# Experts 1 to 7 of a routed layer behind one branch: two arms with different place widths, and tiles with fixed homes

## The chip, the cores and the metric

The kernel runs on one core of one Trainium2 chip. The metric is the device time of one execution in microseconds (us). Three runs of the kernel before gave 397.07, 397.32 and 399.1 us; the median is 397.32 us.

## The reference, cut to what matters

A recurrent attention layer (4 batches, 8 heads, 768 steps, 48 values per head) makes 3072 rows of 384 values. Each row then goes to one of 8 experts, the one with the largest logit:

```python
logits = x @ w_gate                                   # 3072 x 8
expert_idx = np.argmax(logits, axis=1)
gate_w = probs[np.arange(N), expert_idx]              # softmax of the logits
for e in range(8):
    mask = expert_idx == e
    h = np.maximum(x[mask] @ w1[e], 0.0)              # 384 -> 1024
    out[mask] = gate_w[mask, None] * (h @ w2[e])      # 1024 -> 384
```

How many rows an expert gets depends on the data. With the drawn inputs expert 0 gets 394 rows, and the others, sorted, 432, 411, 407, 380, 358, 355 and 335.

## The kernel before, in words

**Attention and routing** (until about 165 us) work through 24 blocks of 128 steps. Each block's rows are ranked within their expert and scattered by POOL into a buffer `xs` in HBM that has a region per expert.

**Expert 0** has 428 places. It is computed in two parts (`Part`, L725), `pa` with 192 places and `pb` with 236. **Experts 1 to 7** are taken in the order of their sorted counts (`sort_experts`, L658), so that the n-th place width in `CAPS` (L32: 428, 464, 432, 416, 408, 392, 384, 384) has to hold the n-th largest count. The program is the same whatever the counts are: it always multiplies all places, and the unused ones hold rows of zeros whose output goes nowhere. `check` (L684) compares the sorted counts with `CAPS` and sets `flag`; where it is set, a slow `general` kernel (L1096) runs behind everything else in an `If` (L1091).

For one expert `load_x` (L916) fetches its rows, `trans_x` (L921) transposes them on PE and splits each value into a high part (ACT) and a low part (DVE), and `mm1` (L943) computes the hidden layer: 8 slices of 128, each 9 matmuls (3 blocks of 384 times high-high, high-low, low-high) whose moving operand is as wide as the expert's places, so 72 matmuls. ACT and DVE then take each slice out of its PSUM bank as a high and a low part (L316, L317); five banks go round. `mm2` (L956) is the second layer, in one of two forms by `shape` (L912):

- **column-wise** (over 384 places): 72 matmuls as wide as the places (L989), the result is output by places, so 12 transposes on PE turn it round (L978), DVE weighs it (L979) and POOL scatters it (L276);
- **row-wise** (384 places, three groups of 128): 24 matmuls for each group (L326), each 384 wide whatever the number of rows, and no transposes behind them.

Before, experts 1 to 5 are column-wise, experts 6 and 7 row-wise. `feed` (L933) splits a piece of weights (`split_piece`, ACT L250, DVE L252) and has SP issue the load of the next piece into one of four staging buffers `wst`.

**Order of the work.** On SP the order is as written, everywhere. On PE, DVE, ACT and POOL it is as written up to L1077, the end of expert 0. From L1078 on a planner orders the instructions of experts 1 to 7 by its own model of time, and may set one of them ahead of what is written before it where its engine would otherwise wait. An engine takes its queue in order. `values_load` (L909, L1085) reads a number from SBUF into a register of an engine: `order` for SP, and `flag` on all five engines, written between `mm1` and `mm2` of expert 7.

The end of expert 0 and the start of expert 1 are, as written:

```python
        for f in range(8):
            pb.mm1(f)
            if f in (1, 4):
                feed(1, f // 3)
        pb.mm2(0)
        trans_x(1)
        feed(1, 2)
        pb.mm2(1)
        feed(1, 3)
    fin = None
    for e in range(1, E):
        expert(e + 2)
```

Of the kernel before, what the change touches and what calls it, by code (L numbers as in the profile page):

```python
# [19 lines left out]
P = 128  # L20
# [9 lines left out]
CAPS = (428, 464, 432, 416, 408, 392, 384, 384)  # L30
NST = 1
# [21 lines left out]
def rwkv_moe_kernel(ctx, tc, rkw, vv, ub, wgp, wg, w1, w2, out):  # L53
# [34 lines left out]
    nth = {"b": 0, "h": 0, "x": 0, "e": 0}  # L88

    def xtile(shape, name):  # L90
        pool, tag = xbanks[nth["x"] % len(xbanks)]
        nth["x"] += 1
        return pool.tile(shape, F32, name=name, tag=tag)
# [96 lines left out]
    flag = const.tile([1, 1], I32, name="flag")  # L190
# [96 lines left out]
    def bank(n, p=P):  # L287
        pool, tag = banks[nth["b"] % len(banks)]
        nth["b"] += 1
        return pool.tile([p, n], F32, name="bank", tag=tag)  # L290

    def h_tiles(n):
        tags = htags[nth["h"] % len(htags)]
        nth["h"] += 1
        if len(tags) == 1:
            t = wk.tile([P, 2, n], F32R, name="hhl", tag=tags[0])
            return t[:, 0, :], t[:, 1, :]
        return [wk.tile([P, n], F32R, name="h" + "hl"[i], tag=g, bufs=wkb.get(g, 2)) for i, g in enumerate(tags)]
# [374 lines left out]
    def check_w():  # L673

        g = sm.tile([RP, NB, NP_ + 1], F32, name="g", tag="g", bufs=1)
        nc.vector.tensor_single_scalar(out=g[:, :, 0:NP_], in_=wtot, scalar=1e3, op=ALU.is_lt)
        nc.vector.tensor_single_scalar(out=g[:, :, NP_:NP_ + 1], in_=chk.unsqueeze(2), scalar=0.0, op=ALU.is_le)
        gm = sm.tile([RP, 1], F32, name="gm", tag="gm", bufs=1)
        nc.vector.tensor_reduce(out=gm, in_=g.rearrange("p n q -> p (n q)"), axis=AX.X, op=ALU.min)
        gb = sm.tile([RP, 1], BF16, name="gb", tag="gb", bufs=1)  # L680
        nc.vector.tensor_copy(gb, gm)
        ch["gb"] = gb

    def check():  # L684
# [12 lines left out]
        any_ = sm.tile([1, 1], F32, name="any", tag="any", bufs=1)  # L697
        nc.vector.tensor_reduce(out=any_, in_=bad, axis=AX.X, op=ALU.max)
# [17 lines left out]
    class Part:  # L716
        def __init__(self, row, rows):
            self.rows = rows
            self.t = ld.tile([rows, 2, XC], F32, name="xg0", tag="rkwt")
            load_rows(self.t, one, row, 2 * rows, rows)  # L720
            x = ld.tile([P, 2, 3, 2 * rows], F32R, name="x0", tag="rkwt")
            self.x = [x[:, i] for i in range(2)]
            self.hs = []
# [187 lines left out]

    def shape(e):  # L912
        n = CAPS[e]
        return (n // P, P) if n <= 3 * P else (4, n // 4)

    def load_x(e):  # L916
        nq, rows = shape(e)
        xg[e] = ld.tile([rows, nq, XC], F32, name="xg", tag="rkwt")
        load_rows(xg[e], eid[e], 0, CAPS[e], rows)

    def trans_x(e):  # L921
        nq, rows = shape(e)
        xh = ld.tile([P, 3, CAPS[e]], F32R, name="xh", tag="rkwt")
        xl = ld.tile([P, 3, CAPS[e]], F32R, name="xl", tag="rkwt")
# [18 lines left out]
    def mm1(e, fin):  # L943
        xh, xl = xhl[e]
        hs = []
        for f in range(8):
            hh, hl = h_tiles(CAPS[e])
            expand(wts[e % 2], f, xh, xl, bank(CAPS[e]), hh, hl)
            hs.append((hh, hl))
            if f == 1 and fin is not None:  # L950
                fin()
            if f in (2, 4, 6):
                feed(e + 1, f // 2 - 1)
        return hs

    def mm2(e, hs):  # L956
        t = xg[e]
        nq, rows = shape(e)
        wt = wts[e % 2]
# [7 lines left out]
        ot = ld.tile([rows, nq, DM], F32, name="ot", tag="rkwt")  # L967
# [14 lines left out]
        for j in range(3):  # L982
            pp = bank(CAPS[e])
# [9 lines left out]
            oT[j] = wk.tile([P, CAPS[e]], F32, name="oT", tag="tmp")  # L993
# [11 lines left out]
    with tc.manual_schedule(engines={ET.PE, ET.DVE, ET.Activation, ET.Pool}):  # L1005
# [11 lines left out]
        psZ = mctx.enter_context(tc.tile_pool(name="psZ", bufs=2, space=PSUM))  # L1017
        banks = [(psZ, "z"), (psZ, "z"), (psW, "w"), (psA, "ap"), (psD, "dp")]
        xbanks[:] = [(psV, "v"), (psX, "tp"), (psX, "tp")]
        nth["x"] = 0  # L1020
        pa.mm1(1)
# [56 lines left out]
    fin = None  # L1078
    for e in range(1, E):
        expert(e + 2)  # L1080
        if e + 1 < E:
            load_x(e + 1)
        hs = mm1(e, fin)
        if e == E - 1:
            bad = nc.values_load(flag[0:1, 0:1], min_val=0, max_val=1)  # L1085
            tc.mark_branch_hint_location("general", "LikelyTaken", [ET.PE, ET.DVE])
        fin = mm2(e, hs)
# [199 lines left out]
```

## Time and profile before

| | us |
|---|---|
| median of 3 runs | 397.32 |
| the profiled execution, its own time | 397.03 |
| span of that execution, first to last instruction | 395.2 |
| PE busy in the span | 376.6 |
| DVE, ACT, POOL busy | 265.9, 233.8, 120.7 |

The span is what the trace shows, and the execution's own time is 1.8 us more. Up to about 165 us no engine alone sets the pace; from there on PE is the engine to look at.

### The profile page before, as it was taken

The page shows a single profiled execution, that of the slowest core. Times are in us where ns is not written, and L with a number is a line of the kernel's source. Part 1 is how long each engine was busy: PE and PEld are TensorE (multiplying, and loading weights), DVE is VectorE, ACT ScalarE, POOL GpSimd, SP SyncE. Part 2 cuts the span into 40 slices and gives each one's busy share as a digit, 9 for nine tenths or more (in the row PEclk, how much of TensorE's full clock was granted, in tenths as well). Part 3 has the DMA queues.
Part 4 walks back from the last instruction along what each step waited for, and adds up shares of the span by engine and source line. Part 5 has one row for each costly group of instructions (what it writes and reads, how often), then busy time and mean ns, then how long its engine had stood idle before and what let it go on. Part 6 is the DMA issues. An engine that isn't in the chain of part 4 may idle for free.

```text
span 395.2 us, 9409 instructions
## 1 busy us (share of the span) xinstructions
PE 376.6 (95%) x3542; PEld 337.3 (85%) x3542; DVE 265.9 (67%) x480; ACT 233.8 (59%) x651; POOL 120.7 (31%) x173
## 2 busy tenths in 40 slices
PE   8798999999998899999999999999999999999994
PEld 6576877777776679898988999999999999999994
DVE  8999899999999986678952661671771762623311
ACT  8899999999999865158543452462452553420200
POOL 5653224775548834001200140030130230312002
PEclk9999999999999999999999999999999999999999
DMA  8999999999921222798937238229228232011001
GB/s 204 205 219 219 283 246 251 230 283 245 245 64 69 96 86 88 194 357 251 294 111 238 80 84 290 81 71 295 80 70 293 80 104 100 18 39 39 18 2 55
DMA packets 30158, 62.04 MB, mean 157 GB/s; under 512 B 4879, under 2 KB 17978, under 8 KB 30108
## 3 DMA queue, kind: packets, MB, share of 16 engines
q1 hardware_dynamic: 25500, 51.92, 48.0%
q0 software_dynamic: 4608, 9.48, 7.5%
q8 instruction: 29, 0.48, 0.6%
q14 instruction: 21, 0.17, 0.1%
HBM read 49.53 MB, written 12.20 MB: 156 GB/s over the span
## 4 chain that ended last, share of the span: by engine, by line
PE 66%; DMA 14%; DVE 11%; ACT 4%; issue 2%; SPq 1%; POOL 0%; POOLq 0%; DVEq 0%; ACTq 0%
PE bank L314 27%; PE bank L989 18%; DMA rkwt<-in_rkw_dram 13%; PE opt L326 10%; DVE at L405 3%; DVE pre L398 2%; DVE suf L382 2%; PE pt L304 2%; PE ap L503 2%; PE op L978 2%; PE yp L539 2%; DVE kh L392 1%; PE lp L553 1%; DMA wst<-in_w_dram 1%; PE yp L516 1%
## 5 line engine op out<-in xcount | busy, mean ns | idle before, releaser
L276 POOL DMA_INDIRECT out_dram<-ot,xg x26 | 30.1, 1156 | 168.9 <-DVE ot L979 126.3
L252 DVE TENSOR_TENSOR w2l<-wst,w2h 128x512 fp32r<-128x512 f32 x48 | 31.0, 683 | 43.6 <-ACT w2h L250 43.6
L314 PE MATMUL bank<-xl,w1h 128*128 128x384 f32 (+5 forms) x168 | 58.7, 352 | 0.0
L314 PE MATMUL bank<-xh,w1l 128*128 128x384 f32 (+5 forms) x168 | 58.4, 350 | 0.0
L314 PE MATMUL bank<-xh,w1h 128*128 128x384 f32 (+5 forms) x168 | 54.1, 354 | 0.0
L316 ACT ACTIVATE hh<-bank 128x384 fp32r<-128x384 f32 (+7 forms) x58 | 26.1, 471 | 37.0 <-PE bank L314 36.5
L376 ACT ACTIVATE at<-ident,ct 128x128 f32<-128x128 f32 x144 | 47.0, 395 | 0.1
L317 DVE SCALAR_TENSOR_TENSOR hl<-bank,hh 128x384 fp32r<-128x384 f32 (+7 forms) x58 | 29.9, 532 | 24.7 <-ACT hh L316 24.4
L349 POOL TENSOR_TENSOR rk<-rkwt 112x512 f32<-112x512 f32 x24 | 31.9, 1330 | 34.9 <-DVE pre L386 28.6
L994 ACT ACTIVATE oT<-bank 128x464 f32<-128x464 f32 (+4 forms) x15 | 7.9, 523 | 48.9 <-PE bank L989 48.9
L503 PE MATMUL ap<-rh,kh 64*128 64x128 f32 (+1 forms) x384 | 27.9, 284 | 7.3 <-DVE rh L359 6.3
L252 DVE TENSOR_TENSOR w1l<-wst,w1h 128x512 fp32r<-128x512 f32 x48 | 31.3, 687 | 4.7 <-ACT w1h L250 4.5
L503 PEld LDWEIGHTS ap<-rh,kh 64*128 64x128 f32 (+1 forms) x384 | 23.3, 187 | 12.6 <-DVE rh L359 9.1
L250 ACT ACTIVATE w1h<-wst 128x512 fp32r<-128x512 f32 x48 | 28.6, 627 | 9.2 <-PE bank L314 4.8
L989 PE MATMUL bank<-hh,w2l 128*128 128x408 f32 (+4 forms) x96 | 34.0, 355 | 0.0
L989 PE MATMUL bank<-hl,w2h 128*128 128x408 f32 (+4 forms) x96 | 33.8, 354 | 0.0
L989 PE MATMUL bank<-hh,w2h 128*128 128x408 f32 (+4 forms) x96 | 33.7, 356 | 0.0
L405 DVE COPY_PREDICATED at<-cmask,ap 128x1024 f32<-128x1024 int32 x24 | 31.6, 1318 | 2.0 <-PE ap L503 1.4
L704 POOL DMA_INDIRECT xs<-xr,pi x24 | 28.4, 1183 | 14.5 <-DVE mx L572 5.5
L382 DVE TENSOR_TENSOR_SCAN suf<-rkwt,sufone 112x520 f32<-112x520 f32 x24 | 31.4, 1307 | 1.4 <-POOL at L364 0.8
L314 PEld LDWEIGHTS bank<-xh,w1l 128*128 128x128 f32 x168 | 31.5, 188 | 0.8
L314 PEld LDWEIGHTS bank<-xl,w1h 128*128 128x128 f32 x168 | 31.4, 188 | 0.7
(173 smaller groups left out, 852.6 us busy)
## 6 DMA issues: line engine op xcount, KB each, us to landing
rkwt<-in_rkw_dram SPq DMA_DIRECT2D x44, 289.5 KB, 9.1
wst<-in_w_dram SPq DMA_DIRECT2D x48, 256.0 KB, 6.6
wst<-in_w_dram SPq DMA_DIRECT2D x16, 768.0 KB, 7.2
vt<-in_vv_dram SPq DMA_DIRECT2D x24, 192.0 KB, 9.1
xg<-xs SPq DMA_DIRECT2D x6, 579.0 KB, 4.7
xs<-zrow SPq DMA_DIRECT2D x8, 289.5 KB, 9.0
rkwt<-in_rkw_dram SPq DMA_DIRECT2D x4, 224.0 KB
xg<-xs SPq DMA_DIRECT2D x1, 675.5 KB
```

The costliest lines, as they stand in the source:

```text
L250: nc.scalar.activation(hi, st[:, cs], AF.Copy)
L252: nc.vector.tensor_tensor(out=lo, in0=st[:, cs], in1=hi.bitcast(F32), op=ALU.subtract)
L276: i = nc.gpsimd.indirect_dma_start(out=out[:, :], out_offset=bass.IndirectOffsetOnAxis(ap=t.bitcast(I32)[:, q, DM + 1:DM + 2], axis=0), in ...
L314: nc.tensor.matmul(hp, a, x[:, j, :], start=(i == 0), stop=(i == 8))
L317: nc.vector.scalar_tensor_tensor(out=hl, in0=hp, scalar=0.0, in1=hh.bitcast(F32), op0=ALU.max, op1=ALU.subtract)
L326: nc.tensor.matmul(op, hs[f][x == "l"][:, cs], w2v(wt, "h" if part == "hl" else "l", f), start=(i == 0), stop=(i == 23))
L349: i = nc.gpsimd.tensor_tensor(out=d["rk"], in0=d["r"], in1=d["k"], op=ALU.mult)
L376: nc.scalar.activation(blk[n]["at"][:, j, q], ident, AF.Copy, scale=blk[n]["ct"][:, head(q, j):head(q, j) + 1])
L382: nc.vector.tensor_tensor_scan(out=suf[:, ::-1], data0=d["w"][:, ::-1], data1=sufone.rearrange("p q c -> p (q c)")[:, ::-1], initial=0.0, ...
L405: nc.vector.copy_predicated(out=d["at"].rearrange("p j q c -> p (j q) c"), mask=cmask.unsqueeze(1).broadcast_to([P, 2 * NP_, C]), data=d[" ...
L503: nc.tensor.matmul(d["ap"][:, j, q, :], d["kh"][rs, q, :], d["rh"][rs, q, :], start=True, stop=True)
L989: nc.tensor.matmul(pp, w, a, start=(i == 0), stop=(i == 23))
```

## The change

`NEAR` is a second list of place widths, smaller than `CAPS`. `check` also compares the sorted counts with `NEAR` and writes a second flag, `far`. Behind expert 0 there is now an `If` with two arms: where some count does not fit, experts 1 to 7 run with `CAPS`, as before; where all fit, they run with `NEAR`. In the second arm experts 5, 6 and 7 (384, 378, 360 places) are row-wise, and row-wise groups have a third of the places. Expert 1's rows are loaded and transposed before the branch, so with 464 places; its `mm1` reads 4 groups of 112 out of 116. Both flags are loaded into registers of all engines before the branch: `far` behind slice 6 of `pb.mm1`, `bad` behind `pb.mm2(0)`. A prefetch hint for PE, DVE and ACT, so far given for the `general` branch, is now given for this branch, directly ahead of it; the `general` branch has none. Since both arms have to find the tiles in the same places, tiles that came from rotating pools (staging, banks, hidden layer, rows, output) now come from `fixed`, which makes each of a ring's tiles once.

The arm that is skipped stands first; with the drawn inputs every count fits `NEAR`, the third one (407) with one place to spare.

```diff
 CAPS = (428, 464, 432, 416, 408, 392, 384, 384)
+NEAR = (428, 448, 424, 408, 396, 384, 378, 360)
...
     def load_piece(e, i):
-        st = wst.tile([P, 1536], F32, name="wst", tag="wst")
+        st = fixed("st", 4, lambda i: wst.tile([P, 1536], F32, name="wst", tag="wst"))
...
+    def fixed(ring, size, make):
+        k = ring, nth[ring] % size
+        nth[ring] += 1
+        if k not in home:
+            home[k] = make(k[1])
+        return home[k]
...
+    def row_tile(rows, *shape, dt=F32, kind=None):
+        n = shape[0] * shape[1]
+        kind = kind or ("rows" if dt == F32 else "cols")
+        t = fixed(kind, {"rows": 3, "cols": 2, "out": 1}[kind], lambda i: ld.tile([P, NW + 2 * NR], dt, name=kind, tag="rkwt"))
+        return t[0:rows, 0:n].rearrange("p (a b) -> p a b", a=shape[0])
...
     def check_w():
 
+        nc.gpsimd.memset(capn, float(1 << 20))
+        for e in range(NST, E):
+            nc.gpsimd.memset(capn[:, e - NST:e - NST + 1], float((NEAR[e] + 1) * E))
...
+        over = sm.tile([1, E], F32, name="over", tag="over", bufs=1)
+        nc.vector.tensor_tensor(out=over, in0=ch["ks"], in1=capn, op=ALU.is_ge)
+        any_ = sm.tile([1, 2], F32, name="any", tag="any", bufs=1)
+        nc.vector.tensor_reduce(out=any_[:, 0:1], in_=bad, axis=AX.X, op=ALU.max)
+        nc.vector.tensor_reduce(out=any_[:, 1:2], in_=over, axis=AX.X, op=ALU.max)
         nc.vector.tensor_copy(flag, any_)
...
     def shape(e):
-        n = CAPS[e]
-        return (n // P, P) if n <= 3 * P else (4, n // 4)
+        n = caps[e]
+        return (3, n // 3) if n <= 3 * P else (4, n // 4)
...
     def mm1(e, fin):
         xh, xl = xhl[e]
+        if caps[e] < CAPS[e] and e == NST:
+            nq, rows = shape(e)
+            xh, xl = (x.rearrange("p j (q r) -> p j q r", q=nq)[:, :, :, 0:rows] for x in (xh, xl))
...
             pb.mm1(f)
             if f in (1, 4):
                 feed(1, f // 3)
+            if f == 6:
+                far = nc.values_load(flag[0:1, 1:2], min_val=0, max_val=1)
         pb.mm2(0)
+        bad = nc.values_load(flag[0:1, 0:1], min_val=0, max_val=1)
         trans_x(1)
         feed(1, 2)
         pb.mm2(1)
         feed(1, 3)
...
+        tc.mark_branch_hint_location("far", "LikelyTaken", [ET.PE, ET.DVE, ET.Activation])
+
+    def experts():
+        fin = None
+        for e in range(1, E):
+            expert(e + 2)
+            if e + 1 < E:
+                load_x(e + 1)
+            hs = mm1(e, fin)
+            fin = mm2(e, hs)
...
+    with tc.If(far > 0, label="far", preferred_fallthrough_block=True) as cmp:
+        experts()
...
+    with cmp.Else():
+        caps[:] = NEAR
+        experts()
     mctx.close()
```

## Rows read from the trace of the kernel before

**Rows 1.** The page: the span, and the chain that ended last, by engine.

```profile
span 395.2 us, 9409 instructions
...
PE 66%; DMA 14%; DVE 11%; ACT 4%; issue 2%; SPq 1%; POOL 0%; POOLq 0%; DVEq 0%; ACTq 0%
```

**Rows 2.** Windows: stretch, length, busy PE, PEld, DVE, ACT, POOL, clock, DMA.

```profile
177.00:189.00 12.00, 11.21 (x68) 10.50 (x68) 9.91 (x20) 9.95 (x19) 1.65 (x1) 1.00 0.89 260
189.00:203.50 14.50, 14.50 (x73) 12.91 (x72) 11.60 (x20) 8.10 (x17) 2.08 (x1) 1.00 0.62 206
```

**Rows 3.** The chain in order of time, experts 1 to 7: start, us, what.

```profile
189.12 8.44 PE bank L314 x40
197.56 0.37 PE pt L304 x4
...
230.04 5.32 PE bank L314 x27
...
260.42 5.12 PE bank L314 x27
...
289.97 5.04 PE bank L314 x27
...
305.39 0.44 PE op L978 x4
...
318.74 4.84 PE bank L314 x27
...
346.89 4.68 PE bank L314 x27
...
377.61 12.14 PE opt L326 x69
```

**Rows 4.** The chain in order of time, end of expert 0.

```profile
182.56 0.62 DVE ort L330
...
183.23 0.62 PE pt L304 x4
183.84 1.10 PE bank L314 x5
184.95 4.17 PE opt L326 x24
```

**Rows 5.** Timeline at the end of expert 0: idle before, releaser in brackets.

```profile
177.60 1.36 ACT L250 ACTIVATE w1h<-wst 128x512 fp32r<-128x512 f32 x2 [0.95 <-DMA wst<-in_w_dram]
...
180.06 0.43 PE L326 MATMUL opt<-w2h,hl 128*118 128x384 f32 x1 [0.25 <-DVE hl L317]
```

**Rows 6.** Line 1091, the branch: ns min/median/max, first and last start (us).

```profile
L1091 SPq EVENT_SEMAPHORE  x9: 17/17/17, 330.1 to 330.7; - x9
...
L1091 SPq COMPARE_BRANCH  x1: 53/53/53, 325.3 to 325.3; - x1
...
L1091 PEldq COMPARE_BRANCH  x1: 482/482/482, 387.1 to 387.1; - x1
L1091 PEldq EVENT_SEMAPHORE  x1: 51/51/51, 389.8 to 389.8; - x1
```

**Rows 7.** DMA queues between 387 and 389.7 us: packets, MB, share.

```profile
q8 instruction: 1, 0.02, 2.7%
```

**Rows 8.** Line 304, window 179 to 184 us, and line 1085: PE's queue.

```profile
L304 PE MATMUL pt<-ident,xg x12: 260/262/319, 181.7 to 183.6; 116*128 116x116 f32 x12
L304 PEldq EVENT_SEMAPHORE  x1: 51/51/51, 180.1 to 180.1; - x1
...
L1085 PEldq TENSOR_LOAD <-flag x1: 539/539/539, 386.4 to 386.4; - x1
```

**Rows 9.** Timeline of SP: the rows of expert 2, and line 270's landing.

```profile
181.94 0.87 SPq L270 DMA_DIRECT2D xg<-xs  x2
...
DMA to landing us min/median/max: 4.7/4.7/4.7
```

**Rows 10.** Timeline of DVE: the low parts of two pieces of weights.

```profile
185.55 1.88 DVE L252 TENSOR_TENSOR w2l<-wst,w2h 128x512 fp32r<-128x512 f32 x3
```

More of the change, by code (lines that the diff above doesn't have):

```diff
@@ L87, in small @@
         return few["t"]
-    nth = {"b": 0, "h": 0, "x": 0, "e": 0}
+    nth = {"b": 0, "h": 0, "x": 0, "e": 0, "rows": 0, "out": 0, "cols": 0, "st": 0, "o": 0}
+    held = []
     def xtile(shape, name):
-        pool, tag = xbanks[nth["x"] % len(xbanks)]
+        i = nth["x"] % len(xbanks)
         nth["x"] += 1
-        return pool.tile(shape, F32, name=name, tag=tag)
+        if not held:
+            return xbanks[i][0].tile(shape, F32, name=name, tag=xbanks[i][1])
+        if len(held) == i + 1:
+            held.append(xbanks[i][0].tile([P, BANK], F32, name="held", tag=xbanks[i][1]))
+        n = shape[1] if len(shape) == 2 else shape[1] * shape[2]
+        t = held[i + 1][0:shape[0], 0:n]
+        return t if len(shape) == 2 else t.rearrange("p (a b) -> p a b", a=shape[1])
     def load(n, part=None):
@@ L189, in rwkv_moe_kernel @@
     early = const.tile([1, 1], F32, name="early")
-    flag = const.tile([1, 1], I32, name="flag")
+    flag = const.tile([1, 2], I32, name="flag")
+    capn = const.tile([1, E], F32, name="capn")
     ebrow = const.tile([1, GB, E], BF16, name="ebrow")
@@ L285, in rwkv_moe_kernel, with bank, make @@
              ("kt", "kt"), ("at",), ("at",)]
[L287 to L290, printed above, removed]
-    def h_tiles(n):
[L293 to L298, printed above, removed]
+    home = {}
+    def fixed(ring, size, make):
[4 more added lines that the diff above has]
+        return home[k]
+    def bank(n):
+        if not held:
+            return banks[0][0].tile([P, n], F32, name="bank", tag=banks[0][1])
+        return fixed("b", len(banks), lambda i: banks[i][0].tile([P, BANK], F32, name="bank", tag=banks[i][1]))[:, 0:n]
+    def h_tiles(n):
+        def make(i):
+            tags = htags[i]
+            if len(tags) == 1:
+                t = wk.tile([P, 2, CMAX], F32R, name="hhl", tag=tags[0])
+                return t[:, 0, :], t[:, 1, :]
+            return [wk.tile([P, CMAX], F32R, name="h" + "hl"[j], tag=g, bufs=wkb.get(g, 2)) for j, g in enumerate(tags)]
+        hh, hl = fixed("h", len(htags), make)
+        return hh[:, 0:n], hl[:, 0:n]
+    def row_tile(rows, *shape, dt=F32, kind=None):
[3 more added lines that the diff above has]
+        return t[0:rows, 0:n].rearrange("p (a b) -> p a b", a=shape[0])
     def transpose_rows(t, nq, rows, xh, xl):
@@ L718, in __init__ @@
             self.rows = rows
-            self.t = ld.tile([rows, 2, XC], F32, name="xg0", tag="rkwt")
+            self.t = row_tile(rows, 2, XC)
             load_rows(self.t, one, row, 2 * rows, rows)
-            x = ld.tile([P, 2, 3, 2 * rows], F32R, name="x0", tag="rkwt")
-            self.x = [x[:, i] for i in range(2)]
+            x = row_tile(P, 6, 2 * rows, dt=F32R)
+            self.x = [x[:, 3 * i:3 * i + 3] for i in range(2)]
             self.hs = []
@@ L965, in ahead @@
                 trans_x(e + 1)
-        ot = ld.tile([rows, nq, DM], F32, name="ot", tag="rkwt")
+        ot = row_tile(rows, nq, DM, kind="out")
         if nq == 3:
@@ L992, in mm2 @@
                     out_tr(j - 1)
-            oT[j] = wk.tile([P, CAPS[e]], F32, name="oT", tag="tmp")
+            oT[j] = fixed("o", 2, out_t)[:, 0:caps[e]]
             nc.scalar.activation(oT[j], pp, AF.Copy)
@@ L1077, in rwkv_moe_kernel, with out_t @@
         feed(1, 3)
[L1078 to L1087, printed above, removed]
+        tc.mark_branch_hint_location("far", "LikelyTaken", [ET.PE, ET.DVE, ET.Activation])
[7 more added lines that the diff above has]
+            fin = mm2(e, hs)
+    def out_t(i):
+        return wk.tile([P, CMAX], F32, name="oT", tag="tmp")
+    for i in range(2):
+        fixed("o", 2, out_t)
+    row_tile(P, 1, 1, kind="out")
+    kept = [(x, x.copy()) for x in (nth, eid, xg, xhl, stg, todo, outs)]
+    with tc.If(far > 0, label="far", preferred_fallthrough_block=True) as cmp:
+        experts()
+    for x, old in kept:
+        if isinstance(x, list):
+            x[:] = old
+        else:
+            x.clear()
+            x.update(old)
+    with cmp.Else():
+        caps[:] = NEAR
+        experts()
     mctx.close()
```

20 lines of the change are left out of this document (10 added, 10 removed).

## The prediction

> **What bounds the kernel now.** I read the page first, for the span and for what the chain that ended last consists of: PE has 66% of it [rows 1]. Then windows over the part that the change touches: in expert 1's first layer PE is busy for all of the 14.50 us at a granted clock of 1.00 (the 2.4 GHz level), while DVE, ACT and the DMA engines have room [rows 2]. Then the chain in order of time: from 189.12 us to the last row-wise matmul, which begins in the stretch at 377.61, it is matmuls and transposes on PE end to end [rows 3]. So experts 1 to 7 are bound by PE, and what they cost is counted in matmuls. The 12 us ahead of them are not: PE idles there in the 177 to 189 us stretch for 12.00 - 11.21 = 0.8 us [rows 2]. Last I read the rows of the only branch that the kernel has today, since the change puts another one in the middle.
>
> **Part 1, narrower places.** The pitch of a matmul is a row's time over its count [rows 3]: 464 columns 8.44 / 40 = 0.211 us, 432: 5.32 / 27 = 0.197, 416: 0.190, 408: 0.187, 392: 0.179, 384: 0.173. Over the columns that is 0.451 to 0.457 ns each, so time goes with the columns, and I take 0.455. Row-wise matmuls are always 384 wide, at 12.14 / 69 = 0.176 us. A column-wise expert has 144 matmuls as wide as its places, a row-wise one 72 such and 72 of 384. Columns saved: expert 1, 144 x 16 = 2304; experts 2 and 3, 144 x 8 = 1152 each; expert 4, 144 x 12 = 1728; expert 5, 1152 (its second layer goes from 392 to 384); expert 6, only its first layer, 72 x 6 = 432; expert 7, 72 x 24 = 1728. Together 9648 columns, at 0.455 ns **4.4 us** less. All of it lies on the path, since PE waits for nothing there. The bounds are 4.3 and 4.5, by the ends of the pitches.
>
> **Part 2, expert 5 row-wise.** Its 12 output transposes go, 0.44 us for four [rows 3]: **1.3 us** less. Its row transposes on the way in fall from 12 to 9 but get wider; four of 108 take 0.37 us [rows 3], so the gain is between nothing and three of them, 0.3 us, and I take nothing, as fewer and wider cancel. The output then leaves by group as for expert 6, beside PE.
>
> **Part 3, what the branch closes off.** Today the planner sets instructions of experts 1 and 2 ahead of the end of expert 0. Five of expert 1's matmuls (1.10 us) run before `pb.mm2(1)` [rows 4]. They now run behind it: moved, not added, as long as PE has no hole in their place. The hole would be the wait for the first transposed block's bank, and I give it 0.2 us (bounds 0 and 0.6, the length of one DVE operation on such a bank, like `ort` [rows 4]). In return two delays go that the planner's early work makes today. ACT waits 0.95 us for a piece of expert 2's weights, so the last slice's low part is late and PE stands 0.25 us [rows 5]. And `ort` starts at 182.56 on DVE although the transposes behind its matmuls run from 181.7 [rows 4, 8]; that is 0.8 us in which DVE works on early weights, and PE's last four transposes wait for it. Together 0.25 + 0.8 - 0.2 = **0.9 us** less (bounds 0 and 1.1).
>
> **Part 4, the branch itself.** Of the branch of today PE's own instruction takes 0.48 us, but from its start at 387.1 to PE's next entry at 389.8 is 2.7 us [rows 6], and one block of instructions is fetched in that time [rows 7]. What covers it is how far PE's queue is ahead of its array. At the end of `pb.mm2(0)`, also 24 matmuls long, the queue stood at the transposes' wait at 180.1 and the first of them ran at 181.7 [rows 8]: 1.6 us ahead. So PE stands for 2.7 - 1.6 = **1.1 us** more. The bounds: nothing, where the queue is further ahead or the hint helps; and 4.8 - 1.6 = 3.2 us if PE's jump costs what SP's does, whose branch at 325.3 is followed by its next entry at 330.1 [rows 6]. I take PE's own row, as the nearest. A gain is excluded, since the branch only adds.
>
> SP, which gets no hint, I charge 4.8 us. It reaches the branch behind the load of expert 2's third piece, whose staging buffer is free when DVE has split expert 1's third piece (1.88 us [rows 10], behind `trans_x`), near 186 us. Behind the branch wait the load of expert 2's rows and then its last piece. The rows are issued near 192 instead of 181.94 and land 4.7 us later [rows 9], near 197. PE wants them, in today's order, behind expert 1's 45th matmul, at 197.56 [rows 3]. So it costs nothing by a hair, and one for one if SP is later.
>
> ACT and DVE, with 4.8 us each at worst, are covered by five PSUM banks: PE first needs one back after 45 matmuls of 448 columns, 45 x 0.204 = 9.2 us. DVE has `ort` (0.62 us) and a piece of weights (1.88) left when PE ends `pb.mm2(1)` [rows 4, 10], and with 4.8 that is 7.3 us. Without that cover PE would stand for the rest. POOL has nothing in expert 1 that anyone waits for.
>
> **Part 5, small things.** Two loads of a flag on each engine: PE's takes 0.54 us [rows 8] and the queue's 1.6 us cover it; on ACT and DVE it runs beside the operation before. Two more operations on DVE in `check` and eight memsets on POOL stand ahead of slices whose banks have the same five-deep cover: nothing. The fixed homes repeat the rings' old sizes (four staging buffers, five banks, ten hidden pairs, three row tiles, two pairs of places), so I see no wait that they add; the single output tile is rewritten half an expert after its scatter. The tail behind the last matmul stays.
>
> **Sum.** Against the profiled execution's own 397.03 us (span 395.2 [rows 1], and 1.8 around it): 397.03 - 4.4 - 1.3 - 0.9 + 1.1 = 391.5. The median of the runs is 0.3 above that execution, so I predict **391.8 us**.
>
> The Trainium skill, "Advanced Engine Details and Errata", section "Control Flow Timing", gives a compare-and-branch about 108 ns. SP's 53 ns and PE's 482 ns for the instruction alone lie on both sides of it, and neither holds the time until the next entry. By that figure alone PE would stand for nothing, and the sum would be 390.7.
>
> **The rivals.**
> - **The branch is free** on PE, because its queue is further ahead or the hint has the block there in time: 391.8 - 1.1 = 390.7, down to 390.0 with the other lower bounds. For it: 24 matmuls of cover; against: the queue was only 1.6 us ahead at the same place [rows 8]. Chance 0.15. By the figure of the Trainium skill ("Advanced Engine Details and Errata", "Control Flow Timing") it would be this case.
> - **The arm starts late on more than one engine.** PE's jump costs as much as SP's (2.1 more), and PE meets the rows or weights of expert 2 late by 1 to 3 us, because the planner's model put them where they would be without the branch's cost: 393.5 to 397. For it: the hair's breadth above. Chance 0.22.
> - **Slower: SP's branch holds the chain.** If SP gets to the branch only when DVE has also split expert 1's fourth piece (behind `ort`, so near 192 us), or its jump waits behind weights in flight, the rows of expert 2 land late and every piece of weights behind them too. What the change saves is 5.5 us net; it turns when they land over 5.5 us behind the place where PE wants them, near 203, and at 207 the time is 401. Against it: that wait needs a buffer order other than the written one. Chance 0.05.
> - **The other arm runs.** Then the widths are as before and only parts 3 and 4 remain: 397.3 + 0.2, no change. The counts of the drawn inputs fit `NEAR`, one of them by a single place. Chance 0.03.
>
> **How the numbers follow.** The forecast's own band, 390.7 to 393.5, has the remaining 0.55. For 8 in 10 the range takes in the free branch down to 390.0 and the late arm up to 395.0. A measurement of this kernel can tell about 0.5%, 2 us, from no change: faster is below 395.3. That holds for the forecast, the free branch and about two thirds of the late arms, 0.85; same gets the rest of these and the other arm, 0.10; slower 0.05.
>
> **What would show it.** Right: first-layer matmuls of 448, 424, 408, 396, 384, 378 and 360 columns at 0.455 ns a column (expert 7's near 0.164 us); L978 with 48 transposes instead of 60; PE without a hole behind the branch but for one of about 1.1 us ahead of expert 1's first matmul; SP silent for several us behind its branch, and no wait of PE for transposed rows of expert 2. Wrong: widths as before; a hole of over 3 us at the branch; PE waiting on banks, rows or weights within expert 1 or 2; or holes later on that fixed homes make.

## The result and the profile after

| | before | after |
|---|---|---|
| median, range (7 runs each) | 397.15 us (396.34 to 399.1) | 401.66 us (399.92 to 403.85) |
| ratio to before, 95% interval | | 1.0105 (1.0071 to 1.014) |
| the profiled execution | 397.03 us, span 395.2 [rows 1] | 400.59 us, span 398.9 |
| end of PE's last matmul | 389.74 us | 393.12 us |

The change made the kernel slower by about 1%, where 391.8 us was predicted. The kernel before took 397.6 us beside the first four experiments and 401.8 to 403.5 us beside the later ones, so kernels are compared by their ratio to the kernel before that was measured beside them, and by stretches of their traces. The attention part varies by some us from one execution to the next; what the change touches is better read from three marks in each trace: the start of the first matmul of `pb.mm1(0)` (expert 0's second part, 236 columns), the start of the last matmul of expert 1's first layer, and PE's end.

| stretch, us | before | after | change | predicted |
|---|---|---|---|---|
| `pb.mm1(0)` to the end of expert 1's first layer | 168.90 to 203.25: 34.35 | 169.98 to 211.31: 41.33 | +6.98 | -0.3 |
| from there to PE's end | to 389.74: 186.49 | to 393.12: 181.81 | -4.68 | -5.2 |
| PE's end to the end of the span | 5.46 | 5.78 | +0.3 | 0 |

The predicted column splits the terms of the prediction: expert 1's first layer loses 72 matmuls x 16 columns x 0.455 ns = 0.5 us, part 3 takes 0.9 and part 4 adds 1.1; the rest of the 5.7 us of parts 1 and 2 lies behind. So the saving behind expert 1 came, and the loss is all in expert 1's first layer. The page says so too. It shows the row of TensorE over 40 slices, and the clock's row below it:

```profile
PE   8798999999998899999939999999999999999994
...
PEclk9999999999999999999969999999999999999999
```

One slice, at 20 x 10 us, has PE at 3 tenths and the clock at 6 tenths. The windows over the same place (columns as in [rows 2]: stretch, length, busy time of PE, PEld, DVE, ACT and POOL, granted clock, DMA share, GB/s) show the hole:

```profile
189.00:203.50 14.50, 10.61 (x53) 9.42 (x51) 8.03 (x14) 4.01 (x9) 2.09 (x1) 0.97 0.69 208
203.50:220.00 16.50, 13.63 (x60) 12.50 (x61) 9.36 (x16) 8.41 (x17) 0.00 (x0) 0.82 0.90 289
...
200.00:203.00 3.00, 0.00 (x0) 0.00 (x0) 0.00 (x0) 0.00 (x0) 0.00 (x0) 0.93 1.03 344
203.00:206.00 3.00, 0.00 (x0) 0.00 (x0) 2.11 (x4) 2.77 (x6) 0.00 (x0) 0.50 1.05 389
206.00:209.00 3.00, 2.63 (x7) 2.37 (x8) 3.00 (x6) 2.64 (x6) 0.00 (x0) 0.50 1.11 357
209.00:210.00 1.00, 1.00 (x5) 0.91 (x5) 1.00 (x3) 0.12 (x1) 0.00 (x0) 0.80 0.94 227
```

Where [rows 2] had PE busy for all of 14.50 us at a clock of 1.00, PE now has 10.61. From 200 to 203 us none of the five compute rows is busy while the DMA engines are full (1.03). And when PE starts again it runs at half clock (0.50, the 1.2 GHz level) until past 209 us. What PE, DVE and ACT waited for stands in their timelines (start, us, engine, line, operation, in brackets the idle time and what ended it), of PE, of DVE and of ACT in turn:

```profile
199.25 0.36 PE L341 MATMUL bank<-cols,w1l 128*128 128x448 f32 x1
206.37 1.11 PE L341 MATMUL bank<-cols,w1h 128*128 128x448 f32 x2 [6.76 <-DVE hl L344]
...
203.89 1.90 DVE L261 TENSOR_TENSOR w2l<-wst,w2h 128x512 fp32r<-128x512 f32 x3 [6.86 <-ACT w2h L259]
205.70 0.62 DVE L344 SCALAR_TENSOR_TENSOR hl<-bank,hh 128x448 fp32r<-128x448 f32 x1
...
194.86 0.52 ACT L343 ACTIVATE hh<-bank 128x448 fp32r<-128x448 f32 x1
203.22 1.67 ACT L259 ACTIVATE w2h<-wst 128x512 fp32r<-128x512 f32 x3 [7.84 <-DMA wst<-in_w_dram]
204.80 0.52 ACT L343 ACTIVATE hh<-bank 128x448 fp32r<-128x448 f32 x1
```

Read from the end: PE has filled the five banks and waits 6.76 us for one. DVE could free it with `hl`, but has ahead of it the low part of a piece of weights, which waits for ACT's high part (6.86 us). ACT stands at that high part, `w2h`, for 7.84 us, because the piece hasn't landed. Slices of expert 1 that PE finished long ago lie behind it in ACT's queue, and `hh` of one of them runs at 204.80, right behind the split. So a piece of **expert 2's** weights, of the second layer, which begins for expert 2 only at 242.87 us, holds **expert 1's** first layer.

Why the piece is late is seen at the branch (L1138), at the order's load behind it (L942) and in SP's timeline; first the rows of line 1138 and of line 942, from 186 to 200 us (ns min/median/max, first and last start):

```profile
L1138 ACTq COMPARE_BRANCH  x1: 68/68/68, 183.9 to 183.9; - x1
L1138 PEldq COMPARE_BRANCH  x1: 393/393/393, 185.4 to 185.4; - x1
L1138 SPq COMPARE_BRANCH  x1: 53/53/53, 187.7 to 187.7; - x1
L1138 DVEq COMPARE_BRANCH  x1: 84/84/84, 188.8 to 188.8; - x1
...
L942 SPq TENSOR_LOAD <-order x1: 1542/1542/1542, 193.2 to 193.2; - x1
```

and SP's timeline:

```profile
187.26 0.38 SPq L248 DMA_DIRECT2D wst<-in_w_dram  x1
195.37 0.89 SPq L279 DMA_DIRECT2D rows<-xs  x2
196.55 0.41 SPq L248 DMA_DIRECT2D wst<-in_w_dram  x1
```

SP's branch begins at 187.7 and its next entry comes at 193.2, 5.5 us later (4.8 in [rows 6]). Expert 2's last piece is issued at 196.55 us and split from 203.22, 6.7 us later. In the kernel before it was the second of these rows, 12.75 us earlier, 1.9 us behind the rows of [rows 9], and ACT split it from 191.38, 7.6 us later. So the load itself is no slower than before; it is issued late. The first row, DVE's, is the last split of expert 2's second piece; it ends at 183.77, and the load goes out right behind it:

```profile
183.09 0.68 DVE L252 TENSOR_TENSOR w1l<-wst,w1h 128x512 fp32r<-128x512 f32 x1
...
183.80 0.40 SPq L239 DMA_DIRECT2D wst<-in_w_dram  x1
```

On PE the branch, which carries a hint, cost nothing. Line 341's row of PE's queue shows the entries behind the branch from 185.8 us, some 0.45 us behind the start of the branch at 185.4, and PE's first matmul of expert 1 runs at 188.46 us right behind the last one of expert 0. So the queue was 3.1 us ahead of the array:

```profile
L341 PEldq EVENT_SEMAPHORE  x5: 51/51/51, 185.8 to 186.2; - x5
```

### The profile page after: what moved, and what is told of

Its sections match the earlier page's. It is cut to its first block, busy times and chain, and to the rows that moved or that the text cites. A ratio compares the mean times of both kernels' runs of the same rounds, so it can differ in the third digit from the quotient of the medians.

```text
span 398.9 us, 9418 instructions
## 1 busy us (share of the span) xinstructions
PE 372.4 (93%) x3527; PEld 334.8 (84%) x3527; DVE 264.9 (66%) x482; ACT 231.7 (58%) x648; POOL 119.6 (30%) x180
## 4 chain that ended last, share of the span: by engine, by line
issue 47%; PE 19%; DVE 16%; POOL 7%; ACT 7%; DMA 2%; POOLq 0%; SPq 0%; DVEq 0%; ACTq 0%; another core or an unknown queue 0%
POOL out_dram L285 6%; PE held L353 4%; PE bank L341 4%; DVE at L432 4%; DVE pre L425 4%; DVE suf L409 3%; PE ap L530 2%; DMA rkwt<-in_rkw_dram 2%; DVE kh L419 2%; ACT at L403 2%; PE lp L580 2%; PE yp L566 1%; PE yq L573 1%; DVE rh L386 1%; PE yp L543 1%
## 5 line engine op out<-in xcount | busy, mean ns | idle before, releaser
L341 PE MATMUL bank<-cols,w1h 128*128 128x192 f32 (+8 forms) x432 | 108.8, 336 | 6.8 <-DVE hl L344 6.8
L341 PEld LDWEIGHTS bank<-cols,w1h 128*128 128x128 f32 x432 | 76.6, 191 | 8.7 <-DVE hl L344 7.1
L285 POOL DMA_INDIRECT out_dram<-out,rows x25 | 29.5, 1178 | 173.6 <-DVE out L1016 62.3
L341 PE MATMUL bank<-cols,w1l 128*128 128x192 f32 (+8 forms) x216 | 71.3, 331 | 0.0
L344 DVE SCALAR_TENSOR_TENSOR hl<-bank,hh 128x192 fp32r<-128x192 f32 (+8 forms) x58 | 29.2, 522 | 25.0 <-ACT hh L343 23.8
L259 ACT ACTIVATE w2h<-wst 128x512 fp32r<-128x512 f32 x48 | 27.9, 626 | 26.3 <-DMA wst<-in_w_dram 15.0
L341 PEld LDWEIGHTS bank<-cols,w1l 128*128 128x128 f32 x216 | 41.2, 191 | 0.6
L425 DVE TENSOR_TENSOR_SCAN pre<-rkwt,pre 112x520 f32<-112x520 f32 x24 | 30.1, 1252 | 0.0
L1026 PE MATMUL bank<-hl,w2h 128*128 128x396 f32 (+3 forms) x78 | 27.4, 354 | 0.0
L1026 PE MATMUL bank<-hh,w2l 128*128 128x396 f32 (+3 forms) x78 | 27.3, 352 | 0.0
```

The lines of the kernel that those rows point to most:

```text
L259: nc.scalar.activation(hi, st[:, cs], AF.Copy)
L285: i = nc.gpsimd.indirect_dma_start(out=out[:, :], out_offset=bass.IndirectOffsetOnAxis(ap=t.bitcast(I32)[:, q, DM + 1:DM + 2], axis=0), in ...
L341: nc.tensor.matmul(hp, a, x[:, j, :], start=(i == 0), stop=(i == 8))
L344: nc.vector.scalar_tensor_tensor(out=hl, in0=hp, scalar=0.0, in1=hh.bitcast(F32), op0=ALU.max, op1=ALU.subtract)
L425: d["ps"] = nc.vector.tensor_tensor_scan(out=pre, data0=d["w"], data1=pre0[n % 2].rearrange("p q c -> p (q c)"), initial=0.0, op0=ALU.mult ...
L1026: nc.tensor.matmul(pp, w, a, start=(i == 0), stop=(i == 23))
```

## The experiments

The theory: the loss comes from SP's jump without a hint together with the planner's order of ACT, in which a split of expert 2's weights stands ahead of slices of expert 1. The rivals: the narrower places, the fixed homes or the row-wise form cost it.

**SP in the hint's list.**

```diff
-        tc.mark_branch_hint_location("far", "LikelyTaken", [ET.PE, ET.DVE, ET.Activation])
+        tc.mark_branch_hint_location("far", "LikelyTaken", [ET.PE, ET.DVE, ET.Activation, ET.SP])
```

> The changed kernel with one more prefetch hint, for SP, which had none. Theory (SP's jump): in the changed kernel SP's branch at 187.70 us is followed by its next entry at 193.20; with the hint that falls to under 1 us, the load of expert 2's last piece of weights (issued at 196.55) goes out about 4.5 us sooner, ACT's wait for it (7.84 us) falls by about that, PE's wait for a bank (6.76 us) to 2 us or less, and the stretch at half clock behind it goes: about 393 to 395 us. Rival (fixed homes of banks and hidden tiles make PE wait): no change, about 401. Rival (the jumps of ACT, DVE or PE): no change, about 401.

397.62 us, ratio 0.9984 (0.9955 to 1.0013): no longer slower than before, and not faster. The expected 393 to 395 us were missed. The first fence has line 1138's and line 942's rows, the second DVE's, SP's, ACT's and PE's timelines in turn:

```profile
L1138 SPq COMPARE_BRANCH  x1: 73/73/73, 187.5 to 187.5; - x1
...
L942 SPq TENSOR_LOAD <-order x2: 273/366/458, 188.0 to 197.2; - x2
```

```profile
188.95 1.88 DVE L261 TENSOR_TENSOR w2l<-wst,w2h 128x512 fp32r<-128x512 f32 x3
...
190.97 0.41 SPq L248 DMA_DIRECT2D wst<-in_w_dram  x1
...
199.08 1.67 ACT L259 ACTIVATE w2h<-wst 128x512 fp32r<-128x512 f32 x3 [2.81 <-DMA wst<-in_w_dram]
...
202.23 0.68 PE L341 MATMUL bank<-cols,w1h 128*128 128x448 f32 x2 [2.83 <-DVE hl L344]
```

With the hint SP's next entry follows 0.5 us behind the branch instead of 5.5, and the piece is issued 5.6 us earlier (190.97 for 196.55). PE's wait falls from 6.76 to 2.83 us but isn't gone: 190.97 is still 7 us later than the 183.80 of before, and ACT's order is the same. It is no longer the branch that holds the piece. SP has issued the rows by 189.8 and then waits for a staging buffer: with fixed homes expert 2's last piece goes where expert 1's last piece lay, and DVE's split of that one ends at 190.83. Before, the piece took the buffer that expert 2's second piece had left at 183.77. From the first mark to the end of expert 1's first layer it takes 37.62 us, so the hint gives back 3.7 us of the 7.0 that were lost.

**The one split moved.** The high part of that piece waits for the last slice of expert 1; ACT's and DVE's orders differ by that, those of PE, SP and POOL don't:

```diff
-                nc.scalar.activation(hi, st[:, cs], AF.Copy)
+                cp = nc.scalar.activation(hi, st[:, cs], AF.Copy)
+                if few.get("late"):
+                    tc.add_manual_dep(cp.ins, few["hh"].name, ..., reason="behind the last slice")
```

> The changed kernel, SP's late jump left as it is; only the split of expert 2's last piece of weights on ACT (and its low part on DVE) is moved behind the last slice of expert 1's first layer. Theory (ACT's queue holds the slices behind a split whose weights come late): PE's wait of 6.76 us goes although SP is as late as before, and with it the half clock: 392 to 394 us. Rival (fixed homes): about 401. Rival (what hurts is the weights themselves being late for PE): PE waits later, in expert 2, about 398 to 401.

400.33 us, ratio 1.0066 (1.0049 to 1.0083), not the 392 to 394 us expected. Expert 1's first layer has no hole (32.93 us from the first mark), but ACT then stands at the next split in its queue, the first of expert 3's weights, which SP issues behind the same jump. ACT's and PE's timelines:

```profile
203.86 0.63 ACT L259 ACTIVATE w1h<-wst 128x512 fp32r<-128x512 f32 x1 [7.36 <-DMA wst<-in_w_dram]
...
208.52 0.74 PE L1026 MATMUL bank<-hh,w2h 128*128 128x448 f32 x1 [5.01 <-DVE hhl L344]
```

PE waits 5.01 us, now in expert 1's second layer. So it isn't this piece alone: ACT's order has later splits, too, ahead of slices that PE waits for, and it fits loads that come earlier than they do.

**The new widths without the branch.** `caps` is set to `NEAR` outright, one copy of experts 1 to 7, fixed homes, no load of the second flag, no hint:

```diff
-    with tc.If(far > 0, label="far", preferred_fallthrough_block=True) as cmp:
-        experts()
...
-    with cmp.Else():
-        caps[:] = NEAR
-        experts()
+    caps[:] = NEAR
+    experts()
```

> The narrow places and the fixed homes with no branch at all: experts 1 to 7 follow expert 0 directly and the other arm is left out, so it is right for these counts only. Theory: the widths bring 4.4 and 1.3 us, and without the branch nothing is lost: about 391 to 392 us. Rival (fixed homes): 396 or more, with waits of PE in several experts.

394.4 us, ratio 0.9906 (0.9883 to 0.9928). PE's windows have no hole (columns as above):

```profile
189.00:203.50 14.50, 14.50 (x77) 13.63 (x76) 9.43 (x17) 6.80 (x14) 3.24 (x2) 1.00 0.76 210
203.50:220.00 16.50, 16.50 (x89) 15.30 (x88) 9.56 (x17) 9.77 (x19) 0.00 (x0) 1.00 0.95 295
```

From the first mark to PE's end it is 388.88 - 173.76 = 215.12 us against 389.74 - 168.90 = 220.84 before: 5.7 us less, which is what parts 1 and 2 add up to. Of it 5.4 us are work that PE no longer has (busy 220.05 us before, 214.64 now), and 0.3 are less waiting. The time itself stayed above the 391 to 392 us expected.

**The branch with the old widths.** The other half: both arms run `CAPS`.

```diff
     with cmp.Else():
-        caps[:] = NEAR
         experts()
```

> The branch, the fixed homes and the loads of the flags, but the arm that runs has the old widths, so expert 5 is column-wise again. Theory: the wait of about 6.8 us and the half clock behind it are all the branch's, the widths only hide part of it: 401.7 + 5.7 = about 407 us, and the same wait of PE in slice 5 or 6 of expert 1. Rival (the narrow widths, by leaving ACT and DVE less time per slice, make the wait): 398 to 400.

406.46 us, ratio 1.0209 (1.0192 to 1.0226): 2% for the branch together with the fixed homes. The waits (engine, line, releaser, us in total, times, longest) name the same chain:

```profile
ACT w2h L259 <- DMA wst<-in_w_dram: 11.4, 2, 8.8
...
PE bank L341 <- DVE hl L344: 7.4, 1, 7.4
```

**Fixed homes alone.** As the run of the new widths without the branch, but with the widths of before.

```diff
-    caps[:] = NEAR
     experts()
```

> Fixed homes alone: the old widths, no branch, no flag load ahead of it, no hint. Theory (the branch with the written-down order of ACT makes the loss): the stretch from pb's first matmul to PE's end is as before, 220.8 us within 1, and the time 397 to 398.5. Rival (fixed homes also cost, hidden in the run without the branch behind the narrower places): over 400, and PE shows gaps of over 0.5 us in experts 1 to 7.

Ratio 1.0014 (0.9964 to 1.0065). From the first mark to PE's end 393.32 - 172.56 = 220.76 us, before 220.84; PE has no gap over 0.6 us. In this order of the work the fixed homes cost no time. But they do make loads late. DVE's and SP's timelines show expert 1's last piece split until 195.22 us, and expert 2's last piece issued right behind that:

```profile
193.33 1.89 DVE L261 TENSOR_TENSOR w2l<-wst,w2h 128x512 fp32r<-128x512 f32 x3
...
195.24 0.40 SPq L248 DMA_DIRECT2D wst<-in_w_dram  x1
```

That is 22.7 us behind the first mark, where the kernel before needs 14.9, the run with SP's hint 21.2 and the change 26.6. So over half of the piece's delay comes with the fixed homes, with or without a branch, and SP's jump adds the last 5 us. Without the branch the planner sets the split behind slices that PE waits for, and the delay costs nothing.

**ACT and DVE in the written order.** Inside both arms the planner leaves ACT and DVE alone; SP's branch stays without a hint:

```diff
-    with tc.If(far > 0, ...) as cmp:
+    with tc.If(far > 0, ...) as cmp, tc.manual_schedule(engines={ET.DVE, ET.Activation}):
...
-    with cmp.Else():
+    with cmp.Else(), tc.manual_schedule(engines={ET.DVE, ET.Activation}):
```

> As the changed kernel, but inside both arms ACT and DVE take their instructions in the order in which they are written, where the splits of the next expert's weights stand among and behind the slices of the hidden layer; SP's branch stays without a hint. Theory (the planner's order of ACT, which sets a split ahead of the slices where SP's jump makes its load late, is the fault): PE's wait of 6.8 us for a bank in expert 1's first layer goes to under 1.5 us, TensorE's granted clock doesn't fall there, and the time is 392 to 396. Rival 1 (SP's late loads are the bound whatever the order): the wait turns up as PE waiting for rows or weights at the start of expert 2, and the time is 399 to 402. Rival 2 (the written order costs elsewhere, as splits stand ahead of slices for other experts): holes spread over experts 2 to 7.

401.61 us beside 403.21 for the kernel before, ratio 0.9968 (0.9922 to 1.0014). The profiled execution ran at half clock from 150 to 165 us, in the attention part (0.50), so only stretches behind it are read. SP is as late as in the change (line 1138 and SP's timeline):

```profile
L1138 SPq COMPARE_BRANCH  x1: 53/53/53, 202.4 to 202.4; - x1
...
211.17 0.41 SPq L248 DMA_DIRECT2D wst<-in_w_dram  x1
```

The last piece is issued 8.8 us behind the branch, as in the change (196.55 - 187.7), and yet expert 1's first layer has no hole: 32.93 us from the first mark. Late loads alone stall nothing there; it takes the planner's order of ACT and DVE as well, so rival 1 falls. Rival 2 is in part right: the waits name one new hole,

```profile
PE held L331 <- DVE out L1016: 1.8, 1, 1.8
```

in front of the last transposes of expert 4's rows, behind its first matmuls.

**The written order and SP's hint.**

```diff
+    ... tc.manual_schedule(engines={ET.DVE, ET.Activation}) in both arms, ET.SP in the hint
```

> As the written order of ACT and DVE in the arms, with SP in the hint's list as well. Theory: both halves of the fault are gone (loads come 5 us earlier, and no split stands ahead of a slice that PE waits for); the stretch from pb's first matmul to PE's end is 215 to 216.5 us, as without the branch, and the time is 393.5 to 395.5, faster than before and at most 1 us above the run without the branch. Rival (order and late loads are one and the same fault, and each mends it alone): no faster than the better of the two single edits.

403.6 us beside 403.21, from four executions, too few for a ratio. By the trace the expected 215 to 216.5 us were missed: 217.83 from the first mark to PE's end, 32.93 of it up to the end of expert 1's first layer, with the same hole as the run before. DVE's and PE's timelines:

```profile
285.88 0.69 DVE L1016 TENSOR_TENSOR out<-held,rows 102x512 f32<-102x512 f32 x1 [6.08 <-DMA out_dram<-out,rows]
...
286.62 0.56 PE L331 MATMUL held<-ident,rows 99*128 99x99 f32 x4 [1.58 <-DVE out L1016]
```

DVE wants to write expert 3's output (102 rows a group) into the one output tile and waits 6.08 us for a scatter of expert 2 to have read it. This is a cost in time of the fixed homes after all, one that this order brings out.

**Two homes for the output tile** (the second in a place of its own), beside the written order and the hint; measured twice, the second time unchanged:

```diff
-        t = fixed(kind, {"rows": 3, "cols": 2, "out": 1}[kind], ...)
+        t = fixed(kind, {"rows": 3, "cols": 2, "out": 2}[kind], ...)
```

> As the run with the written order and SP's hint, and the output tile gets a second home, in a place of its own. Theory (the 1.6 to 1.8 us hole of PE at expert 4's first layer comes from DVE, which waits 6 us for the one output tile until expert 2's and 3's scatters have landed): DVE's wait at L1016 for the scatter and PE's hole are gone, pb's first matmul to PE's end is 214.5 to 216 us instead of 217.8, and the time is at least 1.2% below before, the best of the kernels with the branch. Rival (the hole is the rows' own, or the next thing in DVE's written order holds instead): a hole of over 1 us stays there.

> The run with the written order, SP's hint and two homes for the output tile once more, unchanged, since one of its twelve executions took 1220.77 us. If that was an accident of one execution, none here is over 420 us, and the time is 0.985 to 0.995 of before. Rival (something in this kernel now and then sets the flag behind which the slow general kernel runs): an execution near 1220 us appears again, and a version like this can't be used as it stands.

398.25 us, ratio 0.99 (0.9854 to 0.9945), and 396.33 us, ratio 0.9811 (0.976 to 0.9861): the branch kept, and faster than both kernels. The expected 1.2% was missed by the first and passed by the second, which also lies below the 0.985 to 0.995 expected of the repeat. DVE's wait and PE's hole are gone, and from the first mark to PE's end it is 215.92 and 215.93 us, 0.8 more than without the branch. The windows of the first run (columns as above):

```profile
189.00:203.50 14.50, 14.17 (x73) 13.40 (x74) 9.97 (x18) 7.77 (x17) 3.61 (x2) 1.00 0.70 194
203.50:220.00 16.50, 16.50 (x90) 15.27 (x88) 8.54 (x15) 8.17 (x17) 0.00 (x0) 1.00 0.57 173
```

One of the first twelve executions took 1220.77 us, without a trace; none of the six of the repeat did. Whether it ran the slow `general` kernel, or was held by something else, stays open.

**Expert 5 column-wise, without the branch**, to price the row-wise form; with 388 places, with 392, and with 388 and two homes of the output tile:

```diff
-NEAR = (428, 448, 424, 408, 396, 384, 378, 360)
+NEAR = (428, 448, 424, 408, 396, 388, 378, 360)
```

> Narrower places without the branch, but expert 5 with 388 places and so column-wise (before 392, in the change 384 row-wise). Theory (12 output transposes of 0.11 us and 144 matmuls by 4 columns): 1.3 + 0.3 = 1.6 us more from pb's first matmul to PE's end than in the run without the branch, 216.7 instead of 215.1, and L978's successor shows 60 transposes. Rival (row-wise gains nothing, since its row transposes or its output by groups cost as much): 215.1 to 215.6.

> As the run with expert 5 column-wise at 388 places, but with 392 (four groups of 98 rows in place of 97). Theory (scatters of 97 rows are issued 10 us apart, where 98, 99 and 102 rows take 1.3, so expert 6's output waits for the one output tile): scatters of expert 5 at 1.3 us apart as in the kernel before, no wait of DVE's L357 for a scatter, PE's hole of 6.3 us in expert 7's first layer gone; 216.5 to 217.3 us from pb's first matmul to PE's end, as the row-wise form saves 1.3 and 4 columns 0.3. Rival (column-wise expert 5 ahead of row-wise expert 6 is late in any width): the wait and the hole stay, over 222.

> As the run with expert 5 column-wise at 388 places, with a second home for the output tile. Theory (slow scatters hurt only through the one output tile): the scatters stay 10 us apart, DVE's wait for them at expert 6 goes, and PE's hole of 6.3 us in expert 7 goes or shrinks below 2 us; under 219 us from pb's first matmul to PE's end, but the scatters behind them are late, so that the time from PE's end to the end of the span may grow over 6 us. Rival (slow scatters hold POOL's queue and the chain through something else): the hole stays above 4 us.

With 388 places the ratio is 1.0199 (1.0121 to 1.0276), and the first mark to PE's end 229.0 us, over twelve more than the theory or its rival gave. POOL's, DVE's and PE's timelines, and the DMA queues from 347 to 356 us, show something else:

```profile
346.49 2.17 POOL L285 DMA_INDIRECT out_dram<-out,rows  x1 [22.57 <-DVE out L1016]
356.77 2.16 POOL L285 DMA_INDIRECT out_dram<-out,rows  x1 [8.11 <-issue]
...
377.60 0.62 DVE L357 TENSOR_SCALAR out<-held,rows 126x384 f32<-126x384 f32 x1 [9.76 <-DMA out_dram<-out,rows]
...
378.71 0.67 PE L341 MATMUL bank<-cols,w1h 128*128 128x360 f32 x1 [6.27 <-DVE cols L333]
...
DMA packets 544, 0.14 MB, mean 16 GB/s; under 512 B 514, under 2 KB 514, under 8 KB 544
```

A scatter of 97 rows (388 / 4) goes out in 544 packets at 16 GB/s, and the next one starts 10.3 us later. Expert 6's output waits 9.76 us for the one tile, and PE 6.27 us behind that. With 392 places, POOL's timeline and the DMA queues from 348 to 358 us:

```profile
348.10 0.96 POOL L285 DMA_INDIRECT out_dram<-out,rows  x1 [22.35 <-DVE out L1016]
349.37 0.96 POOL L285 DMA_INDIRECT out_dram<-out,rows  x1 [0.30 <-issue]
...
DMA packets 256, 0.55 MB, mean 55 GB/s; under 512 B 104, under 2 KB 152, under 8 KB 256
```

Scatters of 98 rows start 1.3 us apart, and all four together take 256 packets; the wait and the 6.27 us hole are gone (ratio 1.0026, 0.9979 to 1.0074). With 388 places and two homes the scatters stay 10 us apart and PE's hole in expert 7 goes too (219.15 us from the first mark to PE's end, 0.15 over what was expected; 6.05 us from PE's end to the span's; ratio 1.0154, 1.0022 to 1.0285, too wide to tell more). All three have another hole of PE, of 1.8 to 2.2 us, in front of expert 3's output transposes. In the run with 388 places and one home ACT stands before it at a split that waits 6.79 us for its load. SP, which issues that load, had waited 22.6 us for scatters of expert 2 to land before it could load the rows of expert 5 into the home of expert 2's rows. So the hole has the same form as that of the change, a late load and a split ahead of other work, without a branch. The 219.44 us with 392 places, against 216.5 to 217.3 expected, are 217.4 without it.

The row-wise form is priced from the last matmul of expert 4's first layer to that of expert 6's: 54.88 us row-wise, 56.24 with 388 places, 56.41 with 392. Less the columns (144 x 4 x 0.455 ns = 0.3, and 0.5) it saves 1.1 and 1.0 us; 1.3 was predicted.

## Why the prediction was wrong

**Parts 1 and 2 (-4.4 and -1.3) were right within 0.3 us.** Without the branch PE had 5.4 us less work, the row-wise form giving 1.0 to 1.1 of its 1.3; in the change the stretch behind expert 1's first layer is 4.7 us shorter, as it is with the hint (181.76 us) and without the branch (181.75). It would be 5.05 if four transposes of expert 2's rows, 0.37 us, had not moved into it (197.56 in [rows 3]); 5.2 were predicted. Line 1015 has 48 output transposes, as said.

**Part 3 (-0.9) was worth about half, and its number is met only by luck.** In the written order the stretch up to the end of expert 1's first layer is 32.93 us, 1.42 under before: 0.5 by the columns and 0.9. But 0.37 of the 0.9 are those four transposes, which only moved, and PE's idle time in the stretch fell by 0.4 us, from 0.79 to 0.39. The two delays that were to go, 0.25 and 0.8, are together more than the 0.8 us for which the prediction itself has PE idle there [rows 2]; in front of its last four transposes PE stood 0.55 us.

**Part 4, PE's own jump (+1.1), was too dear: 0.** The rival in which the branch is free was right on this point, for both of its reasons: the queue went on some 0.45 us behind the branch, and it was 3.1 us ahead of the array instead of 1.6. The 2.7 us of [rows 6] were misread. PE's next entry at 389.8 waits for the last matmul, which ends at 389.74 us, and so it shows no cost of the jump.

**Part 4, SP's jump ("costs nothing by a hair"), is the step that failed**, and with it "ACT and DVE ... are covered by five PSUM banks" and, in part 5, that the fixed homes add no wait. The size of the jump was nearly right (4.8 charged, 5.5 measured). But I followed it only to expert 2's rows and to PE. In the change they were issued at 195.37 and not transposed before 221 us, so they were never late. The jump also delays expert 2's last piece of weights, which already comes late by the fixed homes, and I let it out of the sum because PE doesn't need it until expert 2. ACT does: it takes its queue in order, and the planner had set the split ahead of slices whose banks PE wanted back. The five banks cover 9.2 us from 188.46, to about 198, and the one bank that had come back by then a sixth slice, to 199.6; ACT came free at 204.8. The loss is 41.33 - 32.93 = 8.4 us: 6.76 us of PE's wait and some 1.6 us for the matmuls that ran at half clock behind it. Taken from 390.9, which the measured savings alone give (397.03 - 1.42 - 4.68), that is most of the way to 400.6; the rest is a start of expert 0's second part 1.1 us later, in the attention part, and a tail 0.3 us longer.

The rival "SP's branch holds the chain" had the right root, but that its 401 us are close to the measured time is luck, as it took another path: it had PE waiting for expert 2's rows, and it was given 0.05 because that wait wanted a later place for the branch on SP. The wait that came needs ACT's order, which the planner makes anew for the arm and which the trace of before couldn't show. What it did show was that ACT stood at splits for late pieces at the same place (0.95 us in [rows 5]), and I counted that wait as one that the change would take away.

On the hint, rows speak first: SP 5.5 us without it and 0.5 with it, PE some 0.45 us with it, and POOL 0.3 us without it (its branch at 189.6, its next scatter at 189.9). The Trainium skill, "Runtime: NRT & Kernel Launch", "Instruction fetch mechanics", says that a taken branch to a target outside the fetched window stalls the engine for a fetch; SP's rows without a hint agree, and POOL's show no such stall. The Trainium skill, "Advanced Engine Details and Errata", "Control Flow Timing", gives a compare-and-branch about 108 ns; the branch instructions of line 1138 took 45 to 393 ns, and the figure misses what follows them.

## What to carry to other kernels

A branch's cost is not its own time but what the jump makes late on the one engine that nobody covers: here SP, which issues the loads of weights and rows, so it belongs in the hint's list first. Follow each late load to every queue in which an instruction waits for it, and ask what stands behind that instruction; an early split of later weights ahead of work that frees a PSUM bank is harmless only as long as the load is early. The order that helped here keeps later loads' splits behind the slices on the engines that free banks; a planner that has the branch's cost in its model of time might do as well, which was not tried. And a ring of the same size with fixed places is not the same ring: here it made a load wait for another buffer, and the load came 6 to 8 us later.

## What the runs showed of the hardware that was not expected

- **A hint lasts, and what it is worth differs by engine.** The hints are carried out 0.8 to 0.9 us into the span and still serve a branch at 185 us. The `general` branch shows the other side, on line 1152 (after). Before, it had a hint for PE and DVE (none for ACT, other than the section on the change says), and now it has none: PE's branch instruction took 3.9 us instead of 0.48 [rows 6], and DVE's next entry came 3.4 us behind its own branch instead of 0.6. ACT's, without a hint in both kernels, came 0.4 to 0.5 us behind. Why a missing hint costs SP, PE and DVE microseconds and ACT and POOL next to nothing is not shown. At the `general` branch all of it lies at the end of the kernel, and the tail grew by 0.3 us only.

```profile
L1152 PEldq COMPARE_BRANCH  x1: 3934/3934/3934, 389.8 to 389.8; - x1
...
L1152 DVEq COMPARE_BRANCH  x1: 76/76/76, 393.2 to 393.2; - x1
...
L1152 DVEq EVENT_SEMAPHORE  x1: 21/21/21, 396.6 to 396.6; - x1
```

- **A pause costs more than its length.** In the change PE had been idle since 199.6 when its granted clock fell in the stretch up to 203 us, and busy since 206.4 when it rose again in the one from 209; the matmuls between ran at 0.50. With the hint PE waited only 2.83 us, and still had a mean clock of 0.57 in the 4 us from 203.
- **One row more or less can decide what a scatter costs.** Scatters of 98, 99, 102 and 112 rows start 1.25 to 1.6 us apart in most places and 2.9 at most, those of 97 rows 10.2 to 10.9. The change itself has groups of 106 rows (expert 2's 424 places), whose four scatters run on POOL from 264.9 to 277.8 us instead of some 5 us. SP waits 22.7 us for them, with expert 5's rows, as in the runs with expert 5 column-wise (the row below, of its waits from 245 to 285 us); PE doesn't feel it there, but in the written order it was such a scatter that DVE waited 6.08 us for. The DMA engines' mean share while one scatter of 97 rows ran was 0.08, little more than one in 16. The Trainium skill, "DMA: Bandwidth & Descriptors", "Why a DMA increments its semaphore by 16 and not by 1", has a transfer spread over the largest number of engines up to 16 that divides the outer dimension of both its sides, with an exception for some direct copies. For rows that would be one engine for the prime 97 and two for 106. The share at 97 rows agrees; that of 106 rows was not taken apart from the loads beside it, and 102 rows, six engines by that rule, were no slower than 112.

```profile
SPq L279 <- DMA out_dram<-out,rows: 22.7, 1, 22.7
```
